# Attention and MLP on one core: softmax sums merged into one bank, product 3 in product 5's bank, two score chunks in ring banks, and a new written-out order

## The chip, the cores and the metric

The kernel runs on one core of a Trainium2 chip. The metric is the device time of one execution in microseconds, the median over several runs.

## The reference

```python
def _attn_ref(q, k, v, beacon_k, beacon_v):          # B, H, S, D = 8, 8, 576, 64; 16 beacon keys
    k_all = np.concatenate([beacon_k, k], axis=2)
    v_all = np.concatenate([beacon_v, v], axis=2)
    scores = (1.0 / np.sqrt(D)) * np.matmul(q, k_all.transpose(0, 1, 3, 2))
    causal[:, Nb:] = np.triu(np.ones((S, S), dtype=bool), k=1)   # beacons are always seen
    scores = np.where(causal, -1000000000.0, scores)
    a = np.exp(scores - scores.max(-1, keepdims=True))
    a /= a.sum(-1, keepdims=True) + 1e-09
    return np.matmul(a, v_all)

def _moe_ref(x, w_in, w_out):                        # x: 4608 x 512, w_in: 512 x 2048, w_out: 2048 x 512
    h = x @ w_in
    g = h * (1.0 / (1.0 + np.exp(-1.702 * h)))
    return g @ w_out

def reference(**kwargs):
    attn_out = _attn_ref(**attn_kwargs)
    x = attn_out.transpose(0, 2, 1, 3).reshape(B * S, H * D)
    return _moe_ref(x=x, **moe_kwargs)
```

Inputs and output are float32; the kernel computes in float16 with float32 sums.

## The kernel before

**Attention.** The 64 heads are worked in 16 sets of four (`s`, two sets to a batch row). GpSimd's queue loads q and k of a set and VectorE transposes them (`e_turn`, L446). Scores stand transposed, keys on partitions, and the four heads of a set run in four 32-row strips of TensorE at once (`e_qk`, L474). The scores of a set are cut into chunks of at most 512 columns a head (`CHUNKS`, L361 to L376); a chunk is one PSUM tile `s` of four banks, of which there is one, so QK of a chunk waits for the exponentials of the one before (`chunk`, L933). ScalarE takes the exponentials from PSUM into `E` (`e_exp`, L492), all four heads in one instruction; for the first two sets (`SPLIT and s < HS`) the first chunk is done in two. Causal masks follow on `E`: a compare-and-fill on GpSimd, or for the first sets a minimum on VectorE (`e_mask`, L502).

**Softmax sums and values.** The other four PSUM banks are a ring, `u0` to `u3`, that the rest of TensorE's work takes turns in. Value products and column sums (with a tile of ones as weights) run as four 32-column strips, one per head (`e_av`, L565). For the first four sets (`s < EARLY`) the queries are cut in two halves of 288, each with its own sums; for the twelve later ones, which are called whole here, the cut is at `HA = 224`. VectorE first adds the key blocks of a whole set into `zsum` (`e_zadd`, L528), and two ring tiles take the sums: 352 columns of the second part, and 112 + 80 + 32 of the first. Each tile is transposed out of PSUM (`e_z1`), inverted and transposed back (`e_z2`), and multiplies the value products into `xT` (`e_norm`, L600).

**MLP.** The 4608 tokens are ten groups, two of 256 and eight of 512 (L613). The first product of a group (`e_m1`, L619) goes through the ring, 512 columns at a time, and ScalarE's gelu into `g`. Groups 2 to 9 compute the second product by seven quarter products instead of eight: sums of quarters on VectorE (`e_s`, L718, and once for the weights `e_t`), seven products p = 1 to 7 of 16 matmuls each (`e_prod`, L730), and joins on VectorE that add a product out of PSUM to a partial result in `osb` (`e_join`, L757; `products`, L1078), after which SyncE stores a quarter of the result. Groups 7, 8 and 9 do the first product that way too (`fast`, L1146, matmuls at L831).

In `products`, products 4, 5 and 3 each have a ring tile of their own, and product 5 is read by two joins:

```python
        prod(5)
        u4 = join(5, "m", "m", [u3], False)
        c22 = join(5, "u", "u", [c21, u4])
        store(c22, "u", 1, 1)
        prod(3)
        c12 = join(3, "m", "m", [u4])
```

**Order.** All instructions are recorded as operations of a plan (`Plan`, `op`). The order on each engine is written out (`ORDER`, lists of operation numbers); `run` (L150) walks these lists with modelled durations only to give each ring tile its bank and to merge the engines into one sequence. Before the operations named in `FILL` (L312) TensorE gets matmuls on a scrap tile (72 of 112 columns before QK of chunk 0, two in float32 before chunk 1), whose results nobody reads.

Of the kernel before, what the change touches and what calls it, by code (L numbers as in the profile page):

```python
# [17 lines left out]
        76, 100, 115, 118, 120, 106, 138, 141, 143, 108, 155, 111, 152, 129, 161, 158, 122, 131, 164, 167, 134, 127,  # L18
        170, 173, 176, 145, 125, 148, 150, 177, 182, 188, 191, 227, 194, 197, 232, 183, 203, 234, 200, 178, 237, 179,
        206, 258, 241, 209, 184, 263, 185, 212, 265, 213, 248, 246, 268, 214, 215, 401, 251, 253, 272, 218, 404, 275,  # L20
        244, 279, 219, 220, 407, 282, 284, 277, 221, 414, 320, 296, 304, 290, 302, 292, 300, 298, 312, 308, 294, 318,
        314, 310, 306, 316, 426, 435, 423, 343, 338, 339, 340, 433, 431, 438, 344, 345, 359, 349, 341, 464, 346, 350,
        351, 352, 354, 574, 355, 429, 360, 361, 577, 356, 362, 357, 372, 365, 583, 474, 477, 373, 366, 374, 367, 605,
        480, 484, 375, 482, 607, 368, 506, 502, 488, 492, 610, 490, 486, 498, 504, 500, 508, 514, 510, 516, 494, 496,
        512, 534, 593, 596, 535, 536, 539, 540, 550, 541, 542, 537, 742, 545, 546, 547, 548, 603, 745, 551, 552, 553,
        599, 601, 619, 622, 748, 555, 556, 557, 558, 561, 755, 625, 627, 629, 562, 563, 776, 568, 564, 569, 570, 571,
        779, 764, 767, 659, 637, 641, 657, 649, 651, 647, 661, 635, 631, 653, 805, 772, 770, 774, 643, 655, 633, 639,
        645, 679, 680, 815, 818, 700, 681, 682, 684, 701, 915, 690, 685, 686, 691, 692, 702, 918, 687, 693, 695, 703,
        696, 924, 821, 823, 697, 698, 706, 946, 825, 707, 713, 708, 709, 948, 934, 937, 714, 715, 716, 827, 951, 944,
        940, 942, 853, 831, 833, 855, 857, 851, 843, 835, 837, 847, 839, 845, 829, 849, 841, 1083, 960, 963, 875,  # L30
        876, 880, 877, 878, 881, 882, 1086, 968, 966, 970, 883, 1089, 902, 909, 903, 886, 891, 1096, 887, 888, 889,
        892, 893, 1117, 904, 894, 905, 896, 897, 1120, 898, 899, 910, 911, 1105, 1108, 1146, 912, 976, 994, 996, 972,
        978, 1000, 1002, 992, 984, 990, 986, 988, 974, 980, 982, 998, 1168, 1111, 1115, 1159, 1113, 1156, 1025, 1026,
        1020, 1027, 1171, 1021, 1022, 1028, 1023, 1031, 1177, 1032, 1033, 1164, 1166, 1162, 1199, 1034, 1036, 1047,
        1048, 1037, 1201, 1041, 1042, 1038, 1039, 1233, 1049, 1204, 1043, 1044, 1050, 1235, 1237, 1054, 1055, 1056,
        1057, 1239, 1249, 1190, 1241, 1265, 1251, 1242, 1253, 1255, 1187, 1245, 1267, 1258, 1281, 1257, 1269, 1216,
        1195, 1197, 1193, 1213, 1261, 1271, 1285, 1287, 1283, 1273, 1289, 1274, 1219, 1221, 1223, 1334, 1290, 1293,
        1277, 1357, 1335, 1313, 1318, 1314, 1336, 1315, 1319, 1316, 1320, 1321, 1373, 1324, 1325, 1337, 1326, 1329,
        1327, 1361, 1377, 1375, 1330, 1359, 1340, 1331, 1341, 1332, 1363, 1342, 1366, 1365, 1379, 1381, 1347, 1382,
        1348, 1369, 1389, 1385, 1349, 1343, 1395, 1393, 1391, 1405, 1350, 1397, 1398, 1409, 1437, 1407, 1411, 1413,  # L40
        1401, 1414, 1481, 1438, 1417, 1497, 1442, 1443, 1444, 1483, 1439, 1440, 1499, 1487, 1501, 1485, 1458, 1445,
        1459, 1460, 1489, 1513, 1490, 1448, 1453, 1449, 1450, 1451, 1454, 1503, 1455, 1493, 1505, 1461, 1456, 1464,
        1465, 1517, 1515, 1506, 1529, 1519, 1509, 1466, 1471, 1522, 1472, 1473, 1521, 1533, 1467, 1474, 1582, 1525,
        1535, 1537, 1531, 1538, 1561, 1566, 1562, 1541, 1588, 1567, 1589, 1563, 1564, 1568, 1569, 1572, 1590, 1573,
        1574, 1575, 1591, 1577, 1578, 1595, 1579, 1580, 1583, 1584, 1585, 1596, 1597, 1598,
    ],
    "ACT": [
        1, 3, 77, 79, 103, 101, 107, 109, 112, 153, 156, 130, 159, 162, 132, 165, 168, 135, 171, 174, 189, 192, 228,
        195, 198, 233, 235, 201, 204, 238, 180, 207, 259, 210, 264, 186, 266, 269, 216, 402, 405, 408, 222, 417, 415,
        297, 291, 303, 305, 301, 299, 293, 309, 321, 295, 319, 313, 315, 311, 307, 317, 436, 439, 342, 465, 468, 575,  # L50
        578, 584, 587, 606, 608, 503, 507, 489, 491, 493, 487, 499, 505, 509, 515, 517, 495, 501, 511, 497, 513, 611,
        538, 743, 746, 749, 756, 758, 777, 780, 660, 642, 638, 652, 658, 648, 650, 636, 632, 662, 654, 806, 644, 634,
        656, 640, 646, 809, 916, 683, 919, 928, 925, 947, 949, 952, 828, 832, 854, 856, 852, 858, 834, 838, 844, 840,
        836, 846, 830, 848, 850, 842, 1084, 879, 1087, 1090, 1099, 1097, 1118, 1121, 1147, 1150, 977, 995, 997, 973,
        979, 1001, 993, 985, 991, 989, 1003, 975, 981, 987, 983, 999, 1169, 1172, 1024, 1181, 1178, 1200, 1202, 1234,
        1205, 1236, 1238, 1240, 1250, 1252, 1244, 1266, 1254, 1256, 1268, 1248, 1246, 1264, 1270, 1260, 1282, 1262,
        1272, 1286, 1284, 1288, 1276, 1280, 1292, 1294, 1296, 1278, 1358, 1317, 1374, 1378, 1376, 1360, 1362, 1364,
        1372, 1380, 1368, 1370, 1384, 1390, 1386, 1396, 1394, 1406, 1388, 1392, 1410, 1408, 1412, 1404, 1400, 1416,
        1402, 1482, 1418, 1420, 1498, 1484, 1500, 1441, 1486, 1488, 1496, 1492, 1502, 1504, 1494, 1514, 1516, 1508,
        1518, 1520, 1512, 1510, 1530, 1528, 1534, 1524, 1526, 1536, 1532, 1540, 1544, 1542, 1565,  # L60
    ],
    "DVE": [
        73, 74, 75, 97, 98, 99, 80, 81, 82, 78, 116, 105, 87, 104, 117, 102, 121, 119, 139, 140, 144, 142, 157, 154,
        123, 163, 160, 124, 224, 169, 128, 166, 172, 175, 146, 147, 126, 149, 151, 225, 226, 398, 190, 193, 196, 199,
        255, 256, 257, 202, 205, 286, 242, 411, 287, 211, 208, 243, 399, 249, 247, 400, 250, 412, 254, 252, 273, 245,
        274, 280, 276, 413, 281, 285, 283, 278, 289, 461, 288, 462, 419, 580, 420, 463, 326, 327, 328, 421, 322, 92,
        323, 324, 422, 427, 428, 424, 425, 325, 330, 334, 329, 335, 432, 336, 331, 434, 337, 332, 333, 470, 347, 582,
# [40 lines left out]
    ],  # L108
}


class Op:
    __slots__ = (
        "eng", "dur", "deps", "pr", "due", "emit", "kind", "ring", "mode", "lat",
# [4 lines left out]
class Plan:  # L119
# [13 lines left out]
    def op(self, eng, dur, deps, emit, kind="", pr=5, due=0, ring=None, closes=None, mode=None, name="", count=0, table=None):  # L133
        o = Op()
# [1223 lines left out]
```

## Time and profile before

| | |
|---|---|
| median of 3 runs | 324.89 us (324.66 to 325.06) |
| the profiled execution | 324.84 us, of which its span 323.1 |
| TensorE's mean granted clock | 0.992 |
| busy: TensorE matmuls / VectorE / ScalarE / GpSimd | 312.2 / 261.7 / 219.5 / 113.4 us |
| HBM read, written | 37.22 MB, 9.44 MB |
| largest groups on VectorE | joins 56 x 0.683 us; first `zs` sums 12 x 1.313 |
| largest group on ScalarE | exponentials of 2048 columns, 32 x 1.877 us |

Times are microseconds from the start of the span. PE is TensorE's matmul side, PEld its weight loads, DVE is VectorE, ACT ScalarE, POOL GpSimd, SP SyncE. A row such as `L484 PE MATMUL s<-qT,kT 32*128 32x288` names line, engine, operation, output and inputs, and the size; after an arrow in brackets stands what ended the idle time before the row. In the chain of waits each piece has its start, its length and what ran. In the table by windows each engine has its busy time with the number of its instructions, and near the end stands the clock that TensorE was granted.

### The profile page before, as it was taken

The numbers are of one execution on the slowest core, as the hardware profiler recorded it, in microseconds if no ns is written. First come the engines' busy times: TensorE is split into PE (matmuls) and PEld (weight loads), VectorE is DVE, ScalarE is ACT, GpSimd is POOL, SyncE is SP. The second block draws the span as 40 slices with busy tenths as digits, with TensorE's granted clock in tenths as the row PEclk, the third lists the DMA queues.
The fourth block names the chain that finished last, engine by engine and source line by source line (L and its number), as shares of the span: only waits on it lengthen the run. The fifth ranks groups of instructions, "written<-read, shape, count | busy, mean of one in ns | idle before, by whom it ended". The sixth has DMA issues, their size and how long they took to land. (4 is left out here: it accounts for less than half of the span.)

```text
span 323.1 us, 10371 instructions
## 1 busy us (share of the span) xinstructions
PE 312.2 (97%) x4508; PEld 230.0 (71%) x4508; DVE 261.7 (81%) x524; ACT 219.5 (68%) x272; POOL 113.4 (35%) x178
## 2 busy tenths in 40 slices
PE   7689999999999999999999999999999999999994
PEld 7467665644776467745878877646888888888884
DVE  4837798777987989976998889986999895585784
ACT  1676597677767686689767696768778735974830
POOL 8775478190328403871058208600221000000000
PEclk9899999999999999999999999999999999999998
DMA  7999999294423941396019908900111001101112
GB/s 124 163 200 208 206 185 184 54 97 85 123 70 66 185 73 34 53 183 89 2 36 134 189 3 80 176 28 2 37 34 65 4 32 34 67 2 36 65 67 97
DMA packets 58222, 28.85 MB, mean 89 GB/s; under 512 B 41280, under 2 KB 53568, under 8 KB 58176
## 3 DMA queue, kind: packets, MB, share of 16 engines
q0 software_dynamic: 47552, 18.49, 48.4%
q1 hardware_dynamic: 10560, 9.69, 9.3%
q8 instruction: 35, 0.57, 0.7%
q14 instruction: 11, 0.09, 0.1%
q10 hardware_dynamic: 64, 0.01, 0.0%
HBM read 37.22 MB, written 9.44 MB: 144 GB/s over the span
## 5 line engine op out<-in xcount | busy, mean ns | idle before, releaser
L495 ACT ACTIVATE E<-s 128x2048 f16<-128x2048 f32 (+5 forms) x66 | 98.9, 1515 | 41.4 <-PE s L484 40.9
L630 PE MATMUL u<-xT,w 128*128 128x256 f16 (+1 forms) x512 | 87.3, 326 | 0.6 <-ACT g L651 0.5
L516 POOL TENSOR_SCALAR_AFFINE_SELECT E<-E 128x512 f16<-128x512 f16 (+3 forms) x78 | 48.8, 658 | 107.5 <-ACT E L495 94.2
L630 PEld LDWEIGHTS <-w 128*128 128x128 f16 x512 | 49.0, 98 | 34.7 <-issue 1.9
L651 ACT ACTIVATE g<-u 128x512 f16<-128x512 f32 x80 | 43.2, 599 | 15.6 <-PE u L630 15.4
L744 PEld LDWEIGHTS <-g 128*128 128x128 f16 x512 | 48.5, 98 | 7.1 <-issue 0.3
L744 PE MATMUL u<-w,g 128*128 128x256 f16 x384 | 49.9, 273 | 0.0
L760 DVE SCALAR_TENSOR_TENSOR osb<-u,osb 128x512 f32<-128x512 f32 x56 | 37.6, 683 | 13.6 <-PE u L744 11.7
L484 PEld LDWEIGHTS <-kT 32*128 32x128 f16 x1376 | 25.6, 93 | 20.6 <-issue 12.1
L744 PEld LDWEIGHTS <-sA 128*128 128x128 f16 x384 | 36.3, 98 | 5.1 <-issue 0.3
L484 PE MATMUL s<-qT,kT 32*128 32x32 f16 (+20 forms) x1376 | 34.9, 230 | 3.9 <-ACT E L495 2.0
L859 ACT ACTIVATE g<-u 128x512 f16<-128x512 f32 x48 | 26.9, 602 | 12.4 <-PE u L831 6.8
L744 PE MATMUL u<-tB,sA 128*128 128x256 f16 x256 | 34.9, 273 | 0.1
L606 DVE TENSOR_TENSOR xT<-u,rz 128x352 f16<-128x352 f32 (+2 forms) x52 | 25.8, 518 | 7.4 <-PE u L571 7.1
L415 POOL DMA_DIRECT2D vb<-in_v_dram x32 | 27.4, 876 | 2.2 <-DMA qn<-in_q_dram 1.2
L571 PE MATMUL u<-E,vb 128*32 128x352 f16 (+8 forms) x928 | 27.9, 265 | 0.0
L534 DVE TENSOR_TENSOR zs<-zs,E 128x1344 f16<-128x1344 f16 (+2 forms) x36 | 22.6, 628 | 2.3 <-POOL E L516 1.6
L571 PEld LDWEIGHTS <-vb 128*32 128x32 f16 (+1 forms) x928 | 19.8, 97 | 5.5 <-issue 1.5
L455 DVE STREAM_TRANSPOSE kT<-kn 128x576 f32<-128x576 f32 x16 | 20.1, 1258 | 2.3 <-DMA kn<-in_k_dram 1.5
L831 PE MATMUL u<-xT,w 128*128 128x256 f16 x144 | 20.5, 273 | 0.0
L831 PEld LDWEIGHTS <-w 128*128 128x128 f16 x192 | 18.8, 98 | 2.2
L455 DVE STREAM_TRANSPOSE qT<-qn 128x576 f32<-128x576 f32 x16 | 19.9, 1241 | 0.1
(73 smaller groups left out, 397.5 us busy)
## 6 DMA issues: line engine op xcount, KB each, us to landing
out_dram<-osb SPq DMA_DIRECT2D x36, 256.0 KB, 2.3
kn<-in_k_dram POOLq DMA_DIRECT2D x16, 288.0 KB, 6.3
qn<-in_q_dram POOLq DMA_DIRECT2D x16, 288.0 KB, 6.8
vb<-in_v_dram POOLq DMA_DIRECT2D x24, 128.0 KB, 6.6
w<-in_moe_w_in_dram POOLq DMA_DIRECT2D x8, 256.0 KB, 9.6
w<-in_moe_w_out_dram POOLq DMA_DIRECT2D x4, 512.0 KB, 13.8
vb<-in_v_dram POOLq DMA_DIRECT2D x8, 112.0 KB, 5.0
vb<-in_v_dram POOLq DMA_DIRECT2D x8, 80.0 KB, 7.8
```

The lines of the kernel that those rows point to most:

```text
L415: nc.gpsimd.dma_start(out=t[0 : hi - lo, j, h0:h1, :], in_=v[b, h0:h1, lo:hi, :].rearrange("h n d -> n h d"),)
L455: nc.vector.transpose(out=f32(dst.rearrange("p n e -> p (n e)")).rearrange("p (r t) -> p t r", t=TR), in_=f32(src[:, :]).rearrange("p (t c ...
L484: nc.tensor.matmul(sc[:, h, o : o + w], kT[s % NB2][r : r + 32, j * P : (j + 1) * P, d], qT[s % NB2][r : r + 32, a : a + w, d], start=(d = ...
L495: nc.scalar.activation(out=Es[s][:, :, c0:c1], in_=ss[i][:, :, o : o + c1 - c0], func=AFT.Exp, scale=0.125,)
L516: nc.gpsimd.affine_select(out=blk, in_=blk, compare_op=ALU.is_ge, fill=0.0, base=off + (Nb if j == 0 else 0), pattern=[[0, Q], [1, w]], ch ...
L571: nc.tensor.matmul(u[32 * h : 32 * h + 32, a:e], lhs, src[0:kw, h, col : col + e - a], start=first, stop=last,)
L630: nc.tensor.matmul(u[:, o + a - t0 : o + e - t0], w1t[:, kp, nt * P : (nt + 1) * P], xT[:, kp, a % XR : (e - 1) % XR + 1], start=(kp == 0) ...
L651: nc.scalar.activation(out=gts[g][:, n0:n1, 0:w], in_=rings[("m1", g, n0)][:, 0 : n * w].rearrange("p (n w) -> p n w", n=n), func=AFT.Gelu ...
L744: nc.tensor.matmul(u[:, HM * mt : HM * (mt + 1)], lhs[:, n, mt * P : (mt + 1) * P], rhs[:, n, :], start=(n == 0 and mt == 0), stop=(n == H ...
L760: nc.vector.scalar_tensor_tensor(out=osbs[(g, dst)][:, :], in0=rings[("p", g, p)][:, :], scalar=scale_of(g), in1=osbs[(g, src)][:, :], op0 ...
L831: nc.tensor.matmul(u[:, HM * n : HM * (n + 1)], lhs[x][:, (2 * i + n) * P : (2 * i + n + 1) * P], rhs[:, x, :], start=fresh and n == 0 and ...
L859: nc.scalar.activation(out=gts[g][:, n : n + 2, HM * h : HM * (h + 1)], in_=rings[src][:, :].rearrange("p (n w) -> p n w", n=2), func=AFT. ...
```

## The change

There are five edits and a new order.

1. The sums of a whole set go into one ring tile of 288 columns. `ones` grows to 64 columns: 16 to 31 and 48 to 63 are ones, 32 to 47 zeros. Weights `ones[:, 32:64]` put the sums of queries 288 to 575 into the upper 16 rows of each strip, `ones[:, 16:48]` those of queries 0 to 287 into the lower 16, and one transpose, one reciprocal and one transpose back serve the set. For all sets `zt` becomes a single tile.
2. Product 5 comes ahead of product 4, a single join reads it, and product 3 then adds onto the same bank (no start flag), so that one join of 3 and 5 together ends the group: six joins a group instead of seven.
3. Chunks 1 and 2 (`RINGED`) put their four heads into the four ring banks, one bank a head, and take the exponentials head by head; the chunk behind them in the `s` tile waits for the chunk ahead of them alone. Only set 0's first chunk is still done in two.
4. In the plan's walk a mask on GpSimd and a two-input sum on VectorE may not overlap (`port`).
5. `FILL` is replaced by fillers of 256 columns, which go into a free ring bank wherever the walk shows a gap on TensorE in its first 20 us. In the built program these are 34 ahead of QK of chunk 0 and 17 ahead of chunk 1.

All lists in `ORDER` are new, also those of the loads: q of the first set is loaded ahead of k, and the first column block of `w_in` ahead of v.

```diff
@@ Plan.op, Plan.run
+        if eng == "POOL" and name.startswith("mask"):
+            o.port = 2
+        elif eng == "DVE" and name.rstrip("0123456789") in HELD:   # ("s", "zadd", "xsum", "wsum", "t", "mask")
+            o.port = 1
...
+                if o.port:
+                    t = max(t, held[3 - o.port])
@@ the kernel
-    ones = cst.tile([P, 32], F16, tag="ones", name="ones")
+    ones = cst.tile([P, 64], F16, tag="ones", name="ones")
+    zt = cst.tile([P, HF], F32, tag="zt", name="zt")
+    nc.vector.memset(ones[:, 32:48], 0.0)
-    FILL = {"qk0": ((72, 112, F16),), "qk1": ((2, 256, F32),)}
+    FIRST, WARM, COLS = 3800, 20000, 256
-        CHUNKS += [[(s, 0, HF), (s, HF, EHALF)] if SPLIT and s < HS else ...
+        CHUNKS += [[(s, 0, HF), (s, HF, EHALF)] if SPLIT and s < 1 else ...
+    RINGED = (1, 2)
@@ e_qk, e_exp
+        if i in RINGED:
+            ss[i] = [ring_tile(("qk", i, h)) for h in range(Q)]
...
-            out=Es[s][:, :, c0:c1],
-            in_=ss[i][:, :, o : o + c1 - c0],
+            out=Es[s][:, :, c0:c1] if h is None else Es[s][:, h, c0:c1],
+            in_=sall[i][:, :, o : o + c1 - c0] if h is None else ss[i][h][:, o : o + c1 - c0],
@@ av_terms, e_av
-            if half:
-                return [[2, P, 0, S - HA, zsum[s], HA - Z0, True, True, 0]]
             return [
-                [2, P, Z0, HA, zsum[s], 0, True, True, 0],
-                [2, P, 32, Z0, E, 32, True, True, 0],
-                [2, P, 0, 32, E, 0, True, True, 0],
+                [3, P, 0, HF, zsum[s], HF - Z0, True, False, 0],
+                [2, P, Z0, HF, zsum[s], 0, False, True, 0],
+                [2, P, 32, Z0, E, 32, False, True, 0],
+                [2, P, 0, 32, E, 0, False, True, 0],
             ]
...
+                    lhs = ones[0:kw, 32:64] if x == 3 else ones[0:kw, 16:48]
@@ e_z1, e_z2
-        nc.vector.transpose(out=zt[:, 0 : e - a], in_=rings[("av", s, 2, half)][:, 0 : e - a])
+        nc.vector.transpose(out=zt[:, :], in_=rings[("av", s, 2, half)][:, 0:HF])
...
+        n = 1 if s < EARLY else 2
+        w = n * HF
@@ e_prod
-        u = ring_tile(("p", g, p))
+        u = ring_tile(("p", g, {3: 5}.get(p, p)))
-                    start=(n == 0 and mt == 0),
+                    start=(n == 0 and mt == 0 and p not in (3,)),
@@ chunk
-        if i:
-            deps += [exps[(i - 1, n)] for n in range(len(CHUNKS[i - 1]))]
+        if i in RINGED:
+            key = [("qk", i, h) for h in range(Q)]
...
+        elif i:
+            k = max(x for x in range(i) if x not in RINGED)
+            deps += [x for (j, n), x in exps.items() if j == k]
@@ values
-        order = [(2, 1), (2, 0), (0, 0), (0, 1), (1, 1)] if whole else [
+        order = [(2, 0), (0, 0), (0, 1), (1, 1)] if whole else [
@@ products
-        prod(4)
-        c21 = join(4, "u", "b", [u3])
-        store(c21, "b", 1, 0)
-        prod(5)
-        u4 = join(5, "m", "m", [u3], False)
-        c22 = join(5, "u", "u", [c21, u4])
-        store(c22, "u", 1, 1)
-        prod(3)
-        c12 = join(3, "m", "m", [u4])
+        prod(5)
+        c22 = join(5, "u", "b", [u3], False)
+        store(c22, "b", 1, 1)
+        prod(4)
+        c21 = join(4, "u", "u", [c22])
+        store(c21, "u", 1, 0)
+        prod(3, 5, [c22])
+        c12 = join(3, "m", "m", [u3], at=5)
         store(c12, "m", 0, 1)
@@ the loop that emits the operations
-        for n, w, t in FILL.get(o.name, ()):
+        if o.eng == "PE" and o.start < WARM:
+            free = [(max([0] + [c.end for c in plan.closers.get(x, ())]), i) for i, x in enumerate(held)]
+            since, i = min(free)
+            n = int((2.0 if until > FIRST else 1.8) * (o.start - max(until, since + 200)) / COLS)
```

## The prediction

> **What bounds the kernel now.** I read the page first: its engine shares, then its 40 slices.
>
> ```profile
> PE 312.2 (97%) x4508; PEld 230.0 (71%) x4508; DVE 261.7 (81%) x524; ACT 219.5 (68%) x272; POOL 113.4 (35%) x178
> ...
> PE   7689999999999999999999999999999999999994
> PEclk9899999999999999999999999999999999999998
> ```
>
> TensorE is busy everywhere but in the first three slices and the last. A pipelined matmul counts as busy until its modelled end, so I next took the chain of waits that ended last, which from 207 us on is TensorE alone, and read prices off its pieces.
>
> ```profile
> 222.33 1.80 PE u L571 x72
> 224.14 1.85 PE u L744 x16
> 225.99 0.58 PE s L484 x22
> 226.57 2.29 PE u L744 x20
> ...
> 241.01 1.75 PE u L744 x16
> 242.76 0.87 PE u L831 x8
> ```
>
> Sixteen 128x256 matmuls take 1.75 us (0.109 each) when the next matmul uses the same array form (241.01), and 1.85 us when the next has another form (224.14; QK uses a 32-row form, the value products and sums a 32-column form). So a change of form costs 0.10 us; over the trace's starts it is 0.097. A 128x512 matmul costs 0.216 by the same reading.
>
> With these prices TensorE's time adds up. Counting each shape, the 4432 matmuls that are not filler are 285.8 us. The program changes form 153 times: 153 x 0.097 = 14.8. The last matmul starts at 318.8, so 18.2 us are neither: fillers, waits, half clock, and the 1.9 before the first matmul. Summed up to 25 us the same way, 15.1 of the 18.2 lie there; 3.1 are spread over the other 294 us, the largest 0.65 near 69 us (behind ScalarE's table load) and 0.3 at 30 and 86. From the last start to the span's end 4.3 us pass (join, store, closing semaphores). 285.8 + 14.8 + 15.1 + 3.1 + 4.3 = 323.1, the span. The profiled execution is 324.84, 1.7 more, and 0.05 below the median of 324.89.
>
> Third, the start, by windows:
>
> ```profile
> 7.10:10.50 3.40, 2.63 (x46) 2.04 (x44) 3.06 (x5) 1.52 (x2) 3.30 (x5) 1.00 1.58 179
> 10.50:13.90 3.40, 1.59 (x60) 1.25 (x61) 2.88 (x10) 2.25 (x3) 3.13 (x5) 1.00 1.64 154
> 13.90:17.30 3.40, 3.08 (x85) 2.50 (x85) 3.17 (x10) 1.56 (x2) 1.39 (x2) 0.50 1.71 177
> ```
>
> The first number after the length is TensorE's busy time, the third from the end its clock: after 3.40 us with 1.59 busy the clock is halved for the next 3.40. The timeline shows why TensorE idles there: QK and exponentials alternate on one score tile, and ScalarE waits for each.
>
> ```profile
> 14.95 1.45 ACT L495 ACTIVATE E<-s 128x1536 f16<-128x1536 f32 x1 [0.94 <-PE s L484]
> 17.34 1.45 ACT L495 ACTIVATE E<-s 128x1536 f16<-128x1536 f32 x1 [0.94 <-PE s L484]
> ```
>
> **The change, part by part.** *Merged sums.* For 12 of 16 sets the four column sums stream 576 columns before (352+112+80+32) and after (288+176+80+32): no TensorE work saved. VectorE saves: before 0.536 + 0.405 (transposes of 352 and 224), 0.219 + 0.187 (reciprocals), 0.545 + 0.411 (transposes back) = 2.30 us a set; after one 288 transpose 0.477, a reciprocal of 18 at about 0.26 and a 576 transpose at about 0.78 (both extrapolated from the rows just named) = 1.52. 12 x 0.78 = 9.4 us of VectorE, and one ring bank less per set.
>
> *Product 3 in product 5's bank.* Matmuls unchanged; 8 of 56 joins go, 8 x 0.683 = 5.5 us of VectorE. It adds a wait: product 3 may only start when the first join has read product 5 (0.69 plus some 0.09 of semaphores), and everything behind it on TensorE waits too. The changed program puts 1.04, 2.48, 2.51, 1.61, 3.12, 3.06, 2.62 and 2.62 us of other matmuls between them (counted at the prices above), so 0.78 is hidden if the join starts at once. Without cover it would cost 8 x 0.78 = 6.2.
>
> VectorE is not on the chain after 207 us, so its 15 us count only through waits they end. What is sure is the new order: it has 131 changes of form, 22 fewer, the 32-column runs falling from 37 to 29. **22 x 0.097 = -2.1 us**, on TensorE, with nothing to hide behind.
>
> *Sums and POOL's masks kept apart.* No instruction changes. The trace has both cases: a 128x512 mask takes 0.635 alone and up to 1.60 beside a two-input sum, and the sum stretches too (1.11 to 1.55 for 128x1856); all masks together lose 5.5 us. VectorE's sums feed the 3.1 us of late waits, together with ScalarE's tables and DMAs. **Late waits: 3.1 becomes about 1.6, -1.5 us.** Ends: -2.6 (VectorE's and the full-bank waits all go) and +1.5 (the new order's own waits come to half as much again).
>
> *The start.* Two queries' loads go ahead of the keys', but both are needed: QK 0 still starts at about 8.3, chunk 1's transposes still end at 11.3. Fillers: 34 of 256 columns ahead of QK 0, 24 at half clock (0.215) and 10 at 0.109 from 1.9, end at 8.2; 17 more (1.85) end at 11.0. Neither delays anything, but the second set has only 0.3 us to spare. Then, by rows: four exponentials of 512 columns follow one another every 0.49 (row: two 128x512 ACTIVATE take 1.08), so chunk 1 holds ScalarE 2.1 us where the two calls before took 1.94; chunk 2, four of 384, about 1.7 instead of 1.45. In exchange the next chunk's QK is ready each time: set 0's last exponential ends at about 18.5 instead of 20.9. But the four ring banks are full of scores until then, so sums and values start at 16.3, not 12.2, and the first matmuls of the first MLP product at 21.3, not 17.2. Adding up: the fifth such group ends at 26.4 (25.9 at full clock) with 11.0 us of work and changes done, so 15.4 (14.9) is lost, plus some 0.3 for landings that these rows leave out. **15.6 against 15.1: +0.5 us**; ends -0.2 (full clock, no slips) and +2.0.
>
> I take the half clock again for 13.9 to 17.3, since the stretch 10.5 to 13.9 would hold 0.5 of filler and 1.2 of QK = 1.7 busy, nearest to the 1.59 that was followed by it. The Trainium skill (TensorE: Matmul & The Clock Gate, Part 1) has the clock fall after an idle window of its free-running 3.41 us count. By that reading a half-busy window would keep full clock and the start would cost 0.0 instead of +0.5. The 1.59 row speaks against it, so the row decides.
>
> *The end.* The last product still has one join and one store behind it: 0.
>
> Sum: -2.1 - 1.5 + 0.5 = -3.1 on 324.84, so 321.7; I say **321.8** on the median's scale.
>
> **The rivals.** *More comes:* full clock at 14 us (-0.2 for +0.5) and late waits down to 0.5 (-2.6): -2.1 - 0.2 - 2.6 = -4.9, 319.9; 320.0 when nearly all of it comes. For it: the long zs sums and the masks beside them. Against: table loads and DMAs stay, there are 14 table loads in both programs.
>
> *The start eats it:* if the banks full of scores cost +2.0 and late waits stay at 3.1, -2.1 + 2.0 leaves 324.7. For it: work enters TensorE 4 us later, and the banks are the only room for sums, values and fillers. Against: two exponential chunks more are done by 22 us.
>
> *Slower: product 3 waits for the join.* Price: if VectorE has the two longest zs sums (1.313 + 0.934) and a normalisation (0.518) ahead of the join, the join ends 0.78 + 2.77 = 3.55 us after product 5. Against covers of 1.04, 2.48, 2.51, 1.61 and 3.12 in the five groups beside which sums still run this is late by 2.5 + 1.1 + 1.0 + 1.9 + 0.4 = 6.9 us: 321.7 + 6.9 = 328.6. It decides from 3.1 us of lateness on. For it: VectorE is still some 76% busy and runs in a fixed order. Against: the order written down places few sums directly ahead of those joins, and the joins are 0.69 with more than 1 us of cover in each group.
>
> *The change does not do what it says* can only hold for the fillers; the clock case above prices that.
>
> **How the numbers follow.** Forecast 0.66 (own range 320.4 to 323.6), more comes 0.14, the start eats it 0.12, product 3 waits 0.08. A measurement of this kernel tells about 0.2%, 0.65 us, from no change. Faster by more than that: all of the first two, a third of the third, 0.84; same: the rest of the third, 0.08; slower 0.08. The range 320.0 to 324.4 leaves out product 3's case, half of the eaten start, and the far end of the gain.
>
> **What would show it.** After: TensorE's changes of form are fixed by the program, so the last matmul should start near 315.7. Half clock or not at 14 to 17 us shows in the windows; the first L652 group at 21 and set 0's last exponential at 18.5 in the timeline. DVE's busy time should fall to about 247, joins to 48, and masks stay near 0.64. I am wrong if waits of product matmuls on DVE's joins appear, if TensorE's sum of lost time before 25 us exceeds 17, or if late waits exceed 3.

## The result, and the profile after

The changed kernel takes 327.60 us (median of 6 runs, 327.08 to 328.47) against 324.71 for the kernel before on the same chip: a ratio of 1.0091, 95% interval 1.0076 to 1.0106. It is slower by 2.9 us, where a gain of 3.1 us was forecast, and 327.60 lies above the forecast's upper end of 324.4.

The page of the changed kernel, engine shares and two of the 40-slice lines:

```profile
PE 311.7 (96%) x4483; PEld 230.7 (71%) x4483; DVE 247.9 (76%) x481; ACT 220.7 (68%) x277; POOL 114.5 (35%) x178
...
PE   6589999999999999999999999999999999999995
PEclk9969999999999999999999999999999999999999
```

VectorE lost 13.8 us (261.7 to 247.9; 15 had been worked out), and TensorE is the bound as before. At the prices of the prediction TensorE's work is the same 285.8 us, and its 131 changes of form are 12.7 us instead of 14.8. Still its last matmul starts at 321.7 instead of 318.8. The start of a matmul minus all the work and changes ahead of it is what I call lost time: up to 25 us it is **17.9 (before 15.1)**, behind that **5.4 (before 3.2)**. So -2.1 + 2.8 + 2.2 = +2.9 for the last start.

The start by windows that follow the clock's own steps (after the window and its length: PE, PEld, DVE, ACT, POOL busy; third from the end the clock):

```profile
11.99:15.40 3.41, 1.51 (x72) 1.29 (x72) 0.62 (x4) 2.62 (x5) 1.56 (x2) 1.00 1.84 164
15.40:18.81 3.41, 1.83 (x61) 1.36 (x55) 2.59 (x8) 3.24 (x5) 3.23 (x6) 0.50 1.84 179
18.81:22.22 3.41, 3.28 (x84) 2.41 (x88) 2.52 (x8) 1.98 (x3) 3.27 (x7) 0.50 1.31 201
```

TensorE is about half idle from 12 to 19 us, and two windows run at half clock instead of one. The timeline of the same stretch (start, length, engine, line; in brackets the idle time before and what ended it):

```profile
14.89 0.54 PE L503 MATMUL u<-qT,kT 32*128 32x288 f16 x24 [1.81 <-ACT E L514]
...
16.23 0.83 PE L503 MATMUL s<-qT,kT 32*128 32x208 f16 x32 [0.81 <-ACT E L514]
17.00 1.04 PE L594 MATMUL u<-E,ones 128*32 128x288 f16 x24
17.12 1.45 ACT L514 ACTIVATE E<-s 128x1536 f16<-128x1536 f32 x1 [0.17 <-PE s L503]
...
18.94 0.61 PE L594 MATMUL u<-E,vb 128*32 128x288 f16 x12 [0.90 <-DVE rz L615]
...
23.43 0.83 PE L652 MATMUL u<-xT,w 128*128 128x256 f16 x6
```

ScalarE's gap between exponentials is nearly gone up to 19.3 us (0.94 before, 0.17 here), though gaps of 1.04 and 1.74 follow at 20.4 and 23.6. TensorE pays for that: QK of chunk 2 waits 1.8 us for the ring banks, the first sums start at 17.0 (before 12.2), the first value product at 18.9, the first MLP product at 23.4 (before 17.2). The releaser in the fifth row is named as VectorE, whose `rz` ends at 18.91. But the tile `vb` with the beacon values landed only at 18.81, and where it lands early (v_early, below) the same product waits for `zt` alone, which here was done at 18.15.

The chain of waits begins at 92.67 here (the chain before began at 198.90, so ahead of that the two cannot be compared), and it begins on VectorE:

```profile
92.67 0.60 DVE sA L717
93.28 0.77 DVE g L717
94.05 0.60 DVE osb L782
...
95.35 0.59 DVE zs L553
```

From 92.7 to 99.7 us the path runs over VectorE. Around its start, the timelines of GpSimd, VectorE and TensorE:

```profile
88.72 2.05 POOL L535 TENSOR_SCALAR_AFFINE_SELECT E<-E 128x512 f16<-128x512 f16 x2 [2.08 <-ACT E L514]
91.99 1.78 POOL L535 TENSOR_SCALAR_AFFINE_SELECT E<-E 128x320 f16<-128x320 f16 x2 [1.22 <-ACT E L514]
```

```profile
88.75 1.58 DVE L553 TENSOR_TENSOR zs<-E 128x1856 f16<-128x1856 f16 x1
...
93.20 0.85 DVE L717 TENSOR_TENSOR g<-g 128x512 f16<-128x512 f16 x1
```

```profile
96.34 0.38 PE L594 MATMUL u<-zs,ones 128*32 128x288 f16 x8 [0.77 <-DVE zs L553]
```

Masks and two-input sums still overlap: a sum of 1856 columns takes 1.58 (1.11 alone) and one of 512 takes 0.85 (0.42 as a rule). The plan keeps them apart in its modelled times, and nothing in the built program holds an engine to those.

### The profile page after: what moved, and what is told of

Read it like the earlier page. It is cut to its first block, busy times and chain, and to the rows that moved or that the text cites. A ratio compares the mean times of both kernels' runs of the same rounds, so it can differ in the third digit from the quotient of the medians.

```text
span 325.8 us, 10283 instructions
## 1 busy us (share of the span) xinstructions
PE 311.7 (96%) x4483; PEld 230.7 (71%) x4483; DVE 247.9 (76%) x481; ACT 220.7 (68%) x277; POOL 114.5 (35%) x178
## 4 chain that ended last, share of the span: by engine, by line
PE 65%; DVE 3%; ACT 2%; issue 1%; ACTq 0%; DVEq 0%
PE u L766 26%; PE u L652 17%; PE u L853 11%; PE u L594 6%; PE s L503 5%; ACT E L514 2%; DVE osb L782 1%; DVE u L875 0%; ACT L673 0%; DVE kT L470 0%; DVE g L717 0%; DVE zs L553 0%; ACT g L673 0%; DVE sA L717 0%; DVE bkn L455 0%
## 5 line engine op out<-in xcount | busy, mean ns | idle before, releaser
L514 ACT ACTIVATE E<-s 128x2048 f16<-128x2048 f32 (+5 forms) x63 | 95.6, 1532 | 45.1 <-PE s L503 43.4
L535 POOL TENSOR_SCALAR_AFFINE_SELECT E<-E 128x512 f16<-128x512 f16 (+3 forms) x78 | 50.5, 666 | 85.2 <-ACT E L514 80.6
L652 PEld LDWEIGHTS <-w 128*128 128x128 f16 x512 | 49.3, 98 | 32.9 <-issue 1.1
L673 ACT ACTIVATE g<-u 128x512 f16<-128x512 f32 x80 | 43.8, 598 | 16.1 <-PE u L652 15.9
L766 PEld LDWEIGHTS <-g 128*128 128x128 f16 x512 | 48.7, 98 | 6.8
L766 PE MATMUL u<-w,g 128*128 128x256 f16 x384 | 51.2, 273 | 0.0
L782 DVE SCALAR_TENSOR_TENSOR osb<-u,osb 128x512 f32<-128x512 f32 x48 | 32.9, 685 | 15.8 <-PE u L766 14.2
L766 PEld LDWEIGHTS <-sA 128*128 128x128 f16 x384 | 36.4, 98 | 5.4
L881 ACT ACTIVATE g<-u 128x512 f16<-128x512 f32 x48 | 27.4, 596 | 13.5 <-DVE u L875 10.4
L503 PE MATMUL s<-qT,kT 32*128 32x32 f16 (+20 forms) x1328 | 33.7, 230 | 2.6 <-DVE kT L470 1.5
L766 PE MATMUL u<-tB,sA 128*128 128x256 f16 x256 | 35.7, 273 | 0.0
L594 PE MATMUL u<-E,vb 128*32 128x352 f16 (+8 forms) x928 | 29.0, 268 | 2.1 <-DVE rz L615 0.9
L594 PEld LDWEIGHTS <-vb 128*32 128x32 f16 (+1 forms) x928 | 20.7, 98 | 8.1 <-issue 4.4
L717 DVE TENSOR_TENSOR sA<-g 128x512 f16<-128x512 f16 x32 | 13.1, 420 | 12.1 <-ACT g L673 12.1
L853 PE MATMUL u<-xT,w 128*128 128x256 f16 x144 | 20.4, 273 | 0.0
```

The lines of the kernel that those rows point to most:

```text
L503: nc.tensor.matmul(ss[i][h][:, o : o + w], kT[s % NB2][r : r + 32, j * P : (j + 1) * P, d], qT[s % NB2][r : r + 32, a : a + w, d], start=( ...
L514: nc.scalar.activation(out=Es[s][:, :, c0:c1] if h is None else Es[s][:, h, c0:c1], in_=sall[i][:, :, o : o + c1 - c0] if h is None else s ...
L535: nc.gpsimd.affine_select(out=blk, in_=blk, compare_op=ALU.is_ge, fill=0.0, base=off + (Nb if j == 0 else 0), pattern=[[0, Q], [1, w]], ch ...
L594: nc.tensor.matmul(u[32 * h : 32 * h + 32, a:e], lhs, src[0:kw, h, col : col + e - a], start=first, stop=last, skip_group_check=s >= EARLY ...
L652: nc.tensor.matmul(u[:, o + a - t0 : o + e - t0], w1t[:, kp, nt * P : (nt + 1) * P], xT[:, kp, a % XR : (e - 1) % XR + 1], start=(kp == 0) ...
L673: nc.scalar.activation(out=gts[g][:, n0:n1, 0:w], in_=rings[("m1", g, n0)][:, 0 : n * w].rearrange("p (n w) -> p n w", n=n), func=AFT.Gelu ...
```

## The experiments

**Theory A.** The start's order costs 2.8 us (value loads behind a block of `w_in` and a third q; all scores of both sets ahead of the first sums), and the late waits are loads and masks that meet VectorE's queue. **Theory B.** The start is bound by exponentials and full banks, whatever is loaded when, and the late waits belong to the new forms (merged sums, product 3 behind a join). **Theory C.** Half clock is the price of the start.

All runs are in one table. Each ratio is taken against the kernel before on the same chip, with 4 to 12 runs of the kernel. Lost time is counted as above, on one profiled execution of each kernel; the last column counts windows of 3.41 us at half clock before 30 us, from the clock's first record (4.8 to 8.0 us) on.

| kernel | against before, 95% interval | lost to 25 us | lost later | half windows |
|---|---|---|---|---|
| before | 1 | 15.1 | 3.2 | 1 |
| changed | 1.0091 (1.0076 to 1.0106) | 17.9 | 5.4 | 2 |
| v_early | 1.0060 (1.0045 to 1.0074) | 16.7 | 5.9 | 1 |
| k_first | 1.0072 (1.0056 to 1.0087) | 17.7 | 5.6 | 2 |
| v_and_k | 1.0058 (1.0041 to 1.0074) | 16.9 | 6.0 | 2 |
| old_start | 1.0102 (1.0085 to 1.0119) | 19.0 | 4.9 | 4 |
| v_spread | 1.0027 (1.0017 to 1.0036) | 17.1 | 4.5 | 1 |
| v_nomask | 0.9995 (0.9985 to 1.0004) | 17.2 | 3.3 | 2 |
| v_fill | 1.0170 (1.0153 to 1.0187) | 19.8 | 6.1 | 2 |
| old_fill | 1.0182 (1.0148 to 1.0215) | 20.6 | 6.9 | 3 |
| s_fill | 1.0074 (1.0061 to 1.0087) | 18.6 | 4.3 | 1 |
| s_k | 1.0029 (1.0017 to 1.0040) | 16.9 | 4.4 | 2 |
| s_zs | 1.0037 (1.0023 to 1.0051) | 17.5 | 4.2 | 2 |
| s_all | 1.0077 (1.0061 to 1.0093) | 19.0 | 4.1 | 1 |
| s_w2 | 1.0032 (1.0020 to 1.0043) | 17.1 | 5.0 | 2 |
| mix60 | 1.0027 (1.0015 to 1.0038) | 14.7 | 5.4 | 0 |
| mix80 | 0.9996 (0.9987 to 1.0004) | 14.8 | 4.8 | 1 |
| mix80zs | 0.9997 (0.9987 to 1.0007) | 15.1 | 4.3 | 1 |
| **mix91** | **0.9970 (0.9960 to 0.9979)** | 14.6 | 4.1 | 0 |

**v_early, k_first, v_and_k: the loads of the start.**

```diff
 # v_early: ORDER["POOL"] and ORDER["Q"], behind the q and k loads of sets 0 and 1
-  w1[2], q of set 2, v[1], v[4], v[2], v[0], keep, beacon_v, w1[0], v[3], w1[1]
+  keep, beacon_v, v[0], v[1], v[2], w1[0], w1[1], v[3], v[4], w1[2], q of set 2
 # k_first: POOL and DVE
-  q of set 0, k of set 0        ...  turn q, cast beacon k, turn k
+  k of set 0, q of set 0        ...  cast beacon k, turn k, turn q
```

> Edit: the changed kernel with only its order of loads altered at the start: beacon_v and the first value blocks issue right after the second set's k and q, ahead of the first w1 half and of set 2's q; nothing else moves. Theory A (the value loads landing at 15 to 18.8 us hold the first value products and lengthen the half clock): beacon_v lands near 12.6, the wait of 1.13 us at 17.8 goes, the first value product starts by 17.5, one half-clock window instead of two, lost time up to 25 us falls from 17.9 to 16.0-16.6, and the time to 325.7-326.6. Rival B (banks full of scores: the exponentials of both sets decide when sums and values can run, whenever V lands): the first value product moves by less than 0.5 us, lost time up to 25 us stays above 17.4, time 327.0-327.6. In both the late waits stay at about 5.4 us.

> Edit: the changed kernel with set 0's k loaded ahead of its q, and on VectorE bk0's cast and k's transposes ahead of q's, as before the change; nothing else moves. Theory A (the start is one chain through the first scores): first QK product at 8.3 instead of 8.92, all that follows 0.6 us earlier, time 326.8-327.0. Rival B (what follows waits on the exponentials and loads anyway): first QK at 8.3 but the first MLP group moves by less than 0.2 us, time 327.4-327.6.

> Edit: both of the edits before together (value loads ahead of w1 and set 2's q, set 0's k ahead of its q). Theory A: the gains add: lost time up to 25 us 15.5-16.2, first MLP group at 21.5-22.2, time 325.0-326.0. Rival B (scores and exponentials decide): lost time up to 25 us above 17.0, time 326.8-327.5.

v_early, timeline:

```profile
17.48 0.61 PE L596 MATMUL u<-E,vb 128*32 128x288 f16 x12 [0.31 <-DVE zt L606]
...
21.92 1.48 PE L654 MATMUL u<-xT,w 128*128 128x256 f16 x12
```

The first value product moved by 1.5 us and the MLP with it, and lost time fell from 17.9 to 16.7, just short of Theory A's 16.6. One trace says too much here: v_spread, v_nomask, s_w2 and s_zs load the same at the start and lose 17.1 to 17.5. So the value loads cost 0.4 to 1.2 us, and the time fell by 0.3%, about 1.0 us. In k_first QK starts 0.6 us earlier and the ratio hardly moves (1.0072 against 1.0091, intervals that overlap). In v_and_k the two gains do not add: 16.9 lies between the ranges of both theories. The trace of k_first shows one place where such a gain goes:

```profile
65.11 0.82 PE L699 MATMUL u<-w,g 128*128 128x512 f16 x3
66.97 0.38 PE L699 MATMUL u<-w,g 128*128 128x512 f16 x1 [1.04 <-issue]
```

"issue" means that the engine waited for nothing that the profile shows. The table of DMA queues of k_first for 64.3 to 65.5 us has a row that the stretch 57 to 64.3 has not (queue: packets, MB, share of the 16 engines):

```profile
q8 instruction: 1, 0.02, 4.6%
```

That packet of 16 KB (64.50 to 65.38) I take for TensorE's own program: the page of the changed kernel counts 35 of them for its 8966 matmuls and weight loads, so one holds about 256 instructions. TensorE goes on 1.3 to 1.6 us after it has landed, at the same matmul, number 1118, in the changed kernel (0.30 lost), v_early (0.84), k_first (1.20) and v_and_k (1.52). Part of what is gained ahead of it, or all, is waited off there.

**old_start: before's start under the new rest.**

```diff
-    RINGED = (1, 2)
+    RINGED = ()                 # no score chunks in ring banks; set 1 split again; before's FILL
+    # ORDER: every engine as before up to the model's 17 us, then as in the changed kernel
```

> Edit: the changed kernel's forms (merged sums, product 3 in product 5's bank) and its order from about 17 us on, but before's start: no score chunks in ring banks, set 1's first chunk split again, before's two sets of filler products, and before's order of every engine up to the model's 17 us (set 2's q is loaded ahead of the last six w1 loads, since the later order uses it early). If the start is what went wrong and the late waits follow from it: lost time up to 25 us 15.1-16.0, later 3.2 or less, time 322.5-323.7. If the start lost 2.8 us and the late waits of 5.4 us belong to the new order of the rest: time 324.5-325.5. If neither the ring banks nor the start's order is the matter: 327.0 or more.

It is slower than the changed kernel. By the words put down ahead of it, 327.0 or more (328.27 came) would mean that neither ring banks nor the start's order matter. I do not draw that: the cut leaves stretches in which QK and exponentials alternate alone (waits of 1.56 us each at 17.6 and 20.0), half clock holds for four windows, in which each QK chunk takes 0.83 instead of 0.54, and so half an order is an order of its own. mix60, which keeps the order before for longer, decides it below.

**v_fill, old_fill: fillers against half clock.**

```diff
 # v_fill: v_early, ahead of the third and fifth QK chunk
+    nc.tensor.matmul(ss[3][0][:, 384:512], scrap[:, 0:P], scrap[:, 0:P], start=True, stop=True)   # x26, x9
 # old_fill: old_start; 14 of 256 columns ahead of QK chunk 1, 22 of 128 ahead of chunks 4 and 5
```

> Edit: the kernel with the value loads first (v_early), and 35 more filler products of 128 columns into unused columns of a score bank, 26 ahead of the third QK chunk and 9 ahead of the fifth, in the waits of 1.97 us at 12.7 and 0.96 us at 15.0. Theory A (idle TensorE in a window brings the half clock of the next): no half-clock window at all, and lost time up to 25 us falls from 16.7 to 15.2-16.2, time 0.5-1.4 us under v_early. Rival B (exponentials and loads set the start, the half clock lies in waits): the half window goes but the time stays within 0.3 us of v_early. Rival C (the clock does not follow the filler): a half window stays.

> Edit: the kernel with before's start (old_start), and more fillers: 14 products of 256 columns ahead of the second QK chunk and 22 of 128 columns ahead of each of the fifth and sixth. Its half clock lasted from 13.1 to 26.7, four windows. Theory A (the half clock made that start cost 19.0 us by 25 us): at most one half window, lost time up to 25 us 15.5-16.5, time 2.5-3.5 us under old_start, 324.8-325.8. Rival B (the order of chunks and exponentials costs it): lost time up to 25 us stays above 18, time within 1 us of old_start.

Both failed as experiments: a filler into a score tile had to wait for the exponential that reads the tile (3.2 us at 12.8 in v_fill, 1.6 twice in old_fill), and held up QK behind it.

**v_spread and s_w2: fewer loads beside an instruction fetch.**

```diff
 # v_spread: v_early, ORDER["POOL"], between 53 and 60 us
-  k6, k5, q7, mask, mask, q6, mask, k7, mask, k8, v ... v
+  k5, k6, mask, mask, mask, mask, k8, v ... v, q6, k7, q7
 # s_w2: v_spread, with w2[0] and w2[1] moved behind the loads of set 3
```

> Edit: the kernel with the value loads first (v_early), and of the six q and k loads that GpSimd issues between 53 and 60 us, set 5's k goes first and three (set 6's k, set 7's q and k) go behind the last value load of that stretch, about 10 us later. Theory A (so many transfers at once make TensorE's own instruction fetch of 16 KB wait nearly 4 us, and set 5's k comes late for the norm behind its transpose): the fetch that starts at 64.5 us in the changed kernel starts 1.5-2.5 us earlier, the issue gap of 0.84 us near 65 and the wait of 0.53 us near 62 go, time 1.0-1.5 us under v_early. Rival B (the fetch comes when a count of instructions is reached and not sooner): the gap stays or moves, time within 0.4 us of v_early.

> Edit: v_spread with the first two of the four w2 loads issued about 10 us later, next to the other two. Theory A (TensorE's instruction fetches of 16 KB, which start near 16, 22 and 28 us whatever the start does, wait behind the loads): the fetch of 28 us comes 1 us or more earlier, the issue gaps of 0.66 us at 23.7 and 0.42 us at 29.8 shrink by half or more, time 0.4-0.9 us under v_spread. Rival B (a fetch takes these 4 to 5 us as long as any loads are under way): gaps within 0.2 us of v_spread's, time within 0.2 us.

v_spread gained 0.33 points, 1.1 us. Its fetch starts at 61.47 instead of 63.91 (v_early), and the four matmuls that had the gap among them run through:

```profile
64.57 1.04 PE L699 MATMUL u<-w,g 128*128 128x512 f16 x4
```

The wait for set 5's norm went too, and lost time from 60 to 80 us is about 0.1 instead of 1.5. In s_w2 the fetch of 28.05 stayed at 28.05, the gaps became 0.26 (from 0.66, though TensorE goes on at 24.34 in both) and 0.42 (as in v_spread), and a new wait of 0.71 for w2 came at 40.3. At 28 us the edit had not yet emptied the queues. A little later it had, as the DMA column (last but one) shows, v_spread first and then s_w2:

```profile
31.00:32.30 1.30, 1.30 (x15) 1.17 (x13) 1.28 (x4) 0.59 (x1) 1.29 (x2) 1.00 1.17 203
```

```profile
31.00:32.30 1.30, 1.30 (x15) 1.17 (x13) 1.28 (x4) 0.59 (x1) 1.30 (x2) 1.00 0.35 68
```

TensorE reaches the same matmul at 30.26 in both, but the next packet comes at 33.98 in v_spread and at 31.40 in s_w2. So loads in the queues do hold the fetch up.

**v_nomask: what masks cost.** It is v_early with GpSimd's masks of sets 4 to 15 left out, so a part of the computation is missing.

```diff
-        else:
+        elif s < EARLY:
             nc.gpsimd.affine_select(out=blk, ...
```

> Edit: the kernel with the value loads first (v_early), with the masks that GpSimd applies in sets 4 to 15 left out (part of the computation is missing; GpSimd's loads then issue somewhat earlier). Theory A (masks that overlap VectorE's two-input sums stretch both, and that makes the late waits): the zs wait of 0.83 us at 95 goes and the late waits fall by 1.2-2.0 us. Rival B (joins and norms in VectorE's order make them): only the zs wait changes, late waits fall by 0.8 us or less.

The longest sums' group, in v_early and then in v_nomask (instructions | busy, mean ns | idle before and its releaser):

```profile
L555 DVE TENSOR_TENSOR zs<-E 128x1856 f16<-128x1856 f16 x12 | 14.3, 1192 | 3.1 <-POOL E L537 2.5 <-ACT E L516 0.6
```

```profile
L555 DVE TENSOR_TENSOR zs<-E 128x1856 f16<-128x1856 f16 x12 | 13.4, 1115 | 0.8 <-ACT E L516 0.8
```

Late lost time fell from 5.9 to 3.3, more than either theory said: the wait at 95 us went, and those at 87, 99 and 127. The four zs forms together fell from 37.2 to 34.5 us. This prices masks as a whole: the sums are not stretched any more, they also wait no longer for a mask to end, and loads issue earlier. How the 2.6 us divide among these was not tried.

**s_fill, s_k, s_zs, s_all: on top of v_spread.**

```diff
 # s_fill: right behind QK chunk 3 (24) and chunk 2 (9), ahead of the exponential that reads the bank
+    nc.tensor.matmul(ss[i][0][:, 384:512], scrap[:, 0:P], scrap[:, 0:P], start=True, stop=True)
 # s_k: k_first's edit    # s_zs: DVE: zadd5[2], zadd5[3] ahead of join2.6    # s_all: all three
```

> Edit: the kernel with value loads first and the q and k loads spread (v_spread), and 33 more filler products of 128 columns into unused columns of a score bank, 24 right behind the QK chunk ahead of the wait at 12.9 and 9 right behind the next, so that they run before the exponential that reads the bank (in v_fill they had to wait for it). Theory A (a window with TensorE mostly idle brings half clock): no half window between 15 and 20 us; QK and the first sums and values at full speed; lost time up to 25 us 15.8-16.6 instead of 17.1, time 0.5-1.2 us under v_spread. Rival B (the half clock lies in waits for exponentials): no half window, time within 0.3 us of v_spread. Rival C: a half window stays, no gain.

> Edit: v_spread with set 0's k loaded ahead of its q, and its transposes first. Theory A (with the later obstacles gone, the 0.6 us that the first QK product gains reach the end): 0.4-0.6 us under v_spread. Rival B (the exponentials, the half clock or the instruction fetch take it): within 0.2 us of v_spread.

> Edit: v_spread with set 5's last two two-input sums on VectorE moved ahead of the second join of the third token group. Theory A (the wait of 0.83 us at 94 is set by what is queued ahead of the sums): the wait falls to 0.1-0.2 us, time 0.5-0.8 us under v_spread. Rival B (the join is late then and its bank): the wait moves to the products, time within 0.2 us of v_spread.

> Edit: v_spread with all three: the fillers, set 0's k first, set 5's last sums earlier. Theory A (start, fetch and port collisions add up): 323.8-324.6 at before's 324.8, so equal to before or slightly faster. Rival B (the gains eat each other): 325.2-325.7.

s_fill kept the clock up to 18.5 us and still lost 1.5 us more than v_spread by 25 us, which no theory had. Timeline:

```profile
18.32 0.50 PE L596 MATMUL u<-E,ones 128*32 128x48 f16 x13 [1.30 <-issue]
...
24.34 0.53 PE L505 MATMUL s<-qT,kT 32*128 32x192 f16 x21 [1.22 <-issue]
```

Both issue gaps end 1.3 us behind an instruction packet (16.04 to 16.99, 22.07 to 23.02). The first is new; the second is 0.49 in v_spread and ends at the same 24.34. The packets come at 16, 22 and 28 us in v_spread too, so 33 fillers, 66 instructions with their weight loads, take time off the real work. As an estimate, 66 of 256 of a 6 us step is 1.5 us. s_zs removed the wait at 94 and got it back behind the delayed join:

```profile
94.70 1.03 PE L768 MATMUL u<-tB,sA 128*128 128x256 f16 x8 [0.17 <-DVE osb L784]
...
98.08 0.75 PE L596 MATMUL u<-E,vb 128*32 128x352 f16 x20 [0.48 <-DVE osb L784]
```

s_k again gave nothing, and s_all, worse than both of its theories, is s_fill's loss.

**mix60, mix80, mix91, mix80zs: before's order first, the new forms throughout.**

```diff
 # RINGED = (), before's FILL, before's loads; merged sums and product 3 in product 5's bank kept
 # ORDER of every engine: before's up to the model's 60, 80 or 91 us, then the changed kernel's (as in v_spread)
 # mix80zs: mix80 with s_zs's edit
```

> Edit: the changed kernel's forms (merged sums, product 3 in product 5's bank) throughout, but before's start and before's order of every engine up to the model's 60 us (set 0 and 1 without ring banks, before's fillers and loads), and from there the changed kernel's order with the q and k loads spread as in v_spread; 141 form changes against 153 before and 131 after. Theory A (the changed kernel lost its gain in the order of its first 60 us and at the crossing near 63; its forms and its order behind that are worth taking): lost time up to 25 us 15.1-15.6, at 60 us 16.0-16.5, behind that 3.3-3.8 as in v_spread, form changes 1.2 less than before: 323.6-325.0, at or under before's 324.8. Rival B (the late order is as bad whatever comes ahead of it): behind 60 us 5 or more of lost time, 326 or more.

> Edit: as mix60, but with before's order up to the model's 80 us; 141 form changes. Theory A: as mix60, and the crossing from 60 to 80 us as before (1.0 us lost): 323.4-324.8. Rival B: 326 or more.

> Edit: as mix80, with before's order of every engine up to the model's 91 us, 142 form changes; the products and sums that follow then stand further apart. If the wait of 0.82 us at 93.5 (for set 5's two-input sums, queued behind masks and joins) is a matter of the order at that place: it falls below 0.3 us, time 323.9-324.5, under before's by 0.2% or so. If the sums are late whatever stands ahead (VectorE is full there): the same 0.6-0.9 us come out in another wait, time 324.7-325.2.

> Edit: mix80, with set 5's last two two-input sums on VectorE moved ahead of the second join of the third token group, as in s_zs. If the order at that place decides: 0.5-0.8 us under mix80, 324.1-324.4. If VectorE is full there: the wait moves to the products and the values, as it did in s_zs, within 0.2 us of mix80.

With before's start the lost time up to 25 us is 14.6 to 15.1 under the new forms: the forms are not what the start suffered from. What is left is the wait for the zs sums at 93.5 (0.82 in mix60 and mix80). mix80zs moved it and gained nothing, as s_zs did. mix91 has the order before up to this place, and there the sums end in time:

```profile
87.31 1.11 DVE L554 TENSOR_TENSOR zs<-E 128x1856 f16<-128x1856 f16 x1
88.76 1.64 POOL L536 TENSOR_SCALAR_AFFINE_SELECT E<-E 128x512 f16<-128x512 f16 x3 [2.04 <-ACT E L515]
...
92.08 0.94 DVE L554 TENSOR_TENSOR zs<-zs,E 128x832 f16<-128x832 f16 x2
...
93.75 0.38 PE L595 MATMUL u<-zs,ones 128*32 128x288 f16 x8
```

The masks of this stretch fall beside a transpose and a join here, as they do in the kernel before (89.19 to 90.84), and the long sum takes 1.11. In the changed kernel and in mix80 the masks lie on the sums; the long sum and two of 512 columns behind it take 1.1 us longer together than alone, and the wait is 0.77.

mix91 takes 323.74 us against 324.77, and beats both kernels: 142 changes of form (-1.1), 0.5 us less at the start, 0.9 more late. (mix60 with 325.71 lies above Theory A's range and mix80 with 324.91 at its edge.) The new forms run throughout in mix91, so the late waits do not belong to them, and Theory B falls there.

## Why the prediction was wrong

**Changes of form, -2.1: right.** There are 131 of them, 12.7 us at a price that the new trace repeats (0.096 each). Also right are VectorE's 247 us (247.9), 48 joins, 0 at the end, and that product 3 does not wait for its join: no row of the waits has a product matmul (L766) behind VectorE. Of the three signs of being wrong that one stayed away; the other two came, 17.9 against 17 and 5.4 against 3.

**The start, +0.5: mis-sized, +2.8.** Three of its steps failed. The first is "QK 0 still starts at about 8.3": it starts at 8.9, since the second of the two loads lands at 7.39 instead of 6.93 and the beacon cast and its transpose then stand ahead of k's. Chunk 1's transposes end at 12.0 instead of 11.3. k_first shows that this is worth little at the end. The second is "some 0.3 for landings": the first value loads landed at 15.3 to 18.8 instead of 10.0 to 12.6 and cost 0.4 to 1.2 us of lost time. I had checked the landings of q and k only, though the diff shows that the values had moved back in GpSimd's queue. The third is the full banks: I let sums start at 16.3, the first MLP group at 21.3 and set 0's last exponential end at 18.5. They came at 17.0, at 23.4 (21.9 with the values early) and at 19.3. (The sum was also short by 0.1: 15.4 and 0.3 are 15.7.) That is the rival "the start eats it" (+2.0 for the banks), which had a chance of 0.12. mix60 to mix91 take back 2.8 to 3.3 us with before's start, so the new start as a whole is the cause. How much of it is banks, how much the order of chunks and how much the denser instruction stream behind slow fetches stays open.

**Half clock: one window was expected, two came, and it was not the price.** mix80 and mix80zs had one half window and mix60 and mix91 none, on the same order, and lost time up to 25 us is 14.8 and 15.1 against 14.7 and 14.6. Among kernels with the new start, one window or two makes no more difference (v_early 16.7, v_and_k 16.9). Theory C falls for these starts. What half clock costs in old_start, where QK and exponentials alternate alone, is not shown.

**Late waits, 3.1 to 1.6: wrong in sign, 5.4.** I took the plan's rule that masks and sums must not overlap for a fact of the run, and a lighter VectorE for shorter waits. The zs sums did fall from 38.4 us (15.8, 11.2, 7.2, 4.2 by form) to 37.2, but not to the 34.5 that they take without masks, and masks take 0.666 a piece (0.658 before). What counted was the place. At 63 us a norm stands behind a transpose that waits for k, and then comes an instruction fetch: 1.1 us, gone in v_spread. At 87 to 100 us the masks lie on VectorE's sums, VectorE is on the path for 7 us, and 1.5 us are lost from 85 to 100. Before, the masks of this stretch lie beside transposes and joins, and 0.6 us are lost. v_nomask takes these waits away by the masks, and mix91 by the order, without taking a mask out. The "+1.5" end of this term was too near as well; it came to +2.2.

**The rival that ends slower** (product 3 waits for the join) did not happen. Slower came by two terms whose bad ends (+2.0 and +1.5) I had priced one by one and not together; even together with the -2.1 they make only +1.4.

## What to carry to other kernels

A written-out order that a model made is only as good as the model's landings and overlaps: nothing holds the engines to it, so look where each moved load lands and who is queued behind the engine that waits for it. Fewer changes of form on TensorE were a sure gain here (2.1 us), but a smaller one than what the new start cost. Take new forms with the proven order first and move the order over piece by piece, as mix91 did. Filler matmuls are not free even in idle time (s_fill), since each is two instructions that have to be fetched.

## What the runs showed of the hardware

**Instruction fetch.** The profile shows packets of 16 KB, about 256 instructions of TensorE each, on the same DMA engines as the loads. In the kernels with the new start and no fillers beside QK, TensorE's issue gaps up to 70 us fall on matmuls 351, 479 and 1118, counted from 0, and in s_fill on 223 and 351. 223, 351 and 479 are 128 apart, and 128 matmuls with their weight loads are 256 instructions. At 223, 351 and 1118 TensorE goes on 1.2 to 1.6 us after a packet has landed, whatever time that is. With the queues full the packets came 6 us apart (16.0, 22.1, 28.0 in v_spread), and TensorE can be through with 256 instructions of QK and value products sooner: 24 matmuls of a QK chunk, 48 instructions, take 0.54 to 0.64 us, which makes some 3 us, an estimate. The changed kernel has gaps of 0.26, 0.41 and 0.30 at 24.6, 30.4 and 66.5. The 0.41 is the same in eight kernels, and the kernel before has 0.32 at 30.6, 3.8 us behind a packet, so what makes this one is open.

**The clock.** mix91 and mix80, same order of instructions at the start, cut into the clock's own windows:

```profile
8.25:11.67 3.42, 1.92 (x36) 1.38 (x39) 3.04 (x6) 1.94 (x2) 3.37 (x6) 1.00 1.99 160
11.67:15.08 3.41, 2.01 (x94) 1.83 (x89) 2.86 (x11) 2.27 (x3) 1.96 (x3) 1.00 1.23 159
15.08:18.49 3.41, 2.57 (x68) 1.84 (x61) 2.37 (x7) 2.38 (x2) 1.60 (x3) 1.00 1.69 181
```

```profile
10.66:14.08 3.42, 1.49 (x60) 1.29 (x61) 2.90 (x10) 2.12 (x3) 3.32 (x5) 1.00 1.53 151
14.08:17.49 3.41, 3.10 (x85) 2.51 (x85) 3.18 (x10) 1.54 (x2) 1.55 (x3) 0.50 1.71 175
```

In mix91, windows of 1.92 and 2.01 us busy are followed by full clock; those of 1.49 (mix80), 1.51 (changed), 1.59 (before) and 1.70 (v_early, 13.75 to 17.16) are followed by half. Which 3.41 us are counted differs from run to run. A pair of s_fill shows that a single border in busy time does not hold:

```profile
15.07:18.49 3.42, 1.92 (x85) 1.58 (x77) 1.75 (x6) 3.42 (x5) 2.11 (x4) 1.00 1.62 190
18.49:21.90 3.41, 3.15 (x93) 2.27 (x88) 3.02 (x8) 1.89 (x3) 3.38 (x6) 0.50 1.20 201
```

Over all kernels, a window at full clock with 0.98 to 1.70 us busy was followed by half and one with 1.97 or more by full; in between both came (1.79 in mix60 and 1.92 in mix91 kept it, 1.84 in s_all and 1.92 in s_fill lost it). Back from half clock it takes more: 3.05 (k_first) and 2.88 (s_zs) stayed at half, while 2.80 (old_fill) and 3.00 (v_spread) came back. The Trainium skill (TensorE: Matmul & The Clock Gate, Part 1) has the windows free-running, and there these traces agree; it lets the clock fall after an idle window, and there they differ, since 1.70 and even 1.92 busy of 3.41 lost it.

**The shared port.** The Trainium skill (SBUF — State Buffer, Who interferes with whom) says that a VectorE instruction with two SBUF inputs contends with a GpSimd instruction that reads SBUF. The traces agree: 1.58 us for the sum beside a mask at 88.7, and a mean of 1.115 for all twelve where the masks are left out. In these rows the one that starts first keeps its time and the other is late: the mask at 88.72 takes 0.63, the sum that starts 0.03 behind it 1.58, and the next mask, which starts during that sum, 1.46 (0.59 on average in v_nomask).
